# A fused long-convolution and MLP block on one Trainium2 core: the same operations in another sequence

## The chip, the core and the metric

The kernel runs on one core of one Trainium2 chip. Its time is the device time of one execution in microseconds (us). A core has five engines with an instruction queue each: TensorE (PE in the profile, with its weight loads as PEld), VectorE (DVE), ScalarE (ACT), GpSimd (POOL) and SyncE (SP). They run side by side and meet at semaphores only; each executes its own instructions strictly in the order in which they were written. DMA transfers are started by an instruction on SP, ACT or POOL and are then carried out by 16 DMA engines.

## What is computed

```python
x  = A_q                                   # 1 x 2048 x 640, bf16
xn = _layernorm(x)
# A: depthwise 4-tap convolution of k, times v, then a 2048-long convolution by FFT
k_shift = sum over t of k_pad[:, t:t+S, :] * shift_k[:, ks-1-t]
kv = k_shift * v
y  = irfft(rfft(pad(kv)) * rfft(pad(ssm_k)))[:S] + kv * ssm_D
s  = xn * y
# B: MLP 640 -> 1728 -> 640
g  = silu(gelu(xn @ w1 + b1) @ w2 + b2)
return x + s * g
```

## The kernel before

**Tiles.** The 2048 rows are 16 tiles of 128 rows and 640 columns. For the MLP they form four chunks of four tiles (chunk 0 is tiles 0 to 3). The FFT is done by matmuls in two factors, with two round trips through DRAM scratch (`scrK`, `scrU` after the first factor, `scrC` after the products), in 8 groups.

**Operations.** The kernel is a plan of about 700 named operations. Each name is made of a kind and its indices:

- Layer norm of tile i: `bn` (statistics, DVE), `rs0` to `rs5` (the reciprocal root for a group of tiles, POOL: `rs0` is tile 0, `rs1` tile 1, `rs2` tiles 2 and 3, `rs3` tiles 4 to 7, `rs4` 8 to 11, `rs5` 12 to 15), `xn` (normalize, DVE), `xt` (transpose, PE), `xe` (copy out of PSUM, ACT or DVE).
- MLP: `f1_c_r_ft` is one output block of the first matrix (five matmuls of 512 columns; for chunk 0 the first five blocks come in halves), `ge_...` its gelu on ACT with the bias `b1f`, `f1h` and `geh` the half-height last block. `f2_i_h` is half the columns of tile i of the second matrix (14 matmuls of 320 columns), `si_i` its silu on ACT, `gx_i` the product with `xn` on DVE. ACT must load another function table where gelu and silu alternate (line 687).
- Bias: `b1l` is the DMA of the 3.5 KB of `b1` into `b1r`, and `b1c` converts it into `b1f`, which every gelu reads.
- 4-tap convolution: `kv0` to `kv4`, long DVE operations, `kv4_4` the last.
- FFT: `K1_i`, `U1_i` and their remainders `K1r`, `U1r` are the first factor for the filter and for the signal (PE); `Ke`, `Ue`, `Ker`, `Uer` copy them out of PSUM; `Ks`, `Us` store to scratch, `KL`, `UL` load back. `K2`, `U2`, `X2` are the second factor, `Kf`, `Uf` their copies. `pr`, `pq` are the complex products (DVE). `i1`, `i1r` and `ie`, `ir` are the first inverse factor and its copies, `cs` stores to `scrC`, `cl` loads it, `i2` is the last factor, `ym`, `ad` combine on DVE, `os` stores the output.

**What sets the order.** A string `ORDER` lists every operation once. `Plan.emit` walks through it and writes each operation's instructions into the queue of its engine, so the list is the order on each engine. A token is `name/engine@slots`: after the slash an engine other than the default one (A is ACT, D is DVE, G is POOL, S is SP; N stays on PE but issues each matmul as two of 64 output rows), after the at sign the numbers of the PSUM banks and other buffers that the operation takes:

```python
for token in tokens:
    ...
    o = self.by_name[name]
    e = code[e] if e else o.engs[0]
    ...
    if o.func is not None and o.func != self.table:
        if o.func is not ACT.Sin:
            preload(o.func)
    ...
    o.fn(e)
```

An operation that takes a bank waits for the last reader of that bank. DMAs of SP and ACT share eight completion semaphores in turn, so that a DMA waits for the one eight places before it. `wu0` to `wu5` are four matmuls each on a zero tile, which occupy PE before data has arrived.

In the list of before, `b1l/A` is the first token, `b1c/D` stands behind the first four `xe`, and `rs1`, `rs2`, `rs0` behind `rs3` on POOL.

Of the kernel before, what the change touches and what calls it, by code (L numbers as in the profile page):

```python
# [700 lines left out]
f1_1_0_0@0 kl2 xn0 gte1/A kv0_1a f1_1_0_7@1 xe1/A w2l1 ge_1_0_0 Da xt0@3 sm3 f1_0_1_1@4.1 kv0_2m@0 xe0/A f1h_1@5  # L701
ge_1_0_5 f1h_0@7 ge_1_0_7 kv0_2a f1_0_1_0/N@2 ge_0_1_1 f1_0_0_2/N@0 geh_1 f1_0_0_8/N@3 ge_0_1_0 kv0_3m@0 ge_0_0_2
geh_0 f1_0_0_5/N@6 vl1 ge_0_0_8 kv0_3a K1r_2@4.2 K1_9@0 K1_11@2 Ke_9/A f1_0_0_6@7 vl3 kv0_4 Ker_2/A f1_1_0_4@0 Ke_11/A
kv1_0@0 K1_10@4 f1_0_0_3@1 ge_0_0_6 f1_1_0_1@2 bn14 ge_0_0_3 ge_1_0_4 kv1_1m@1 f1_0_1_2@3 Ke_10/A f1_0_1_3@7 ge_0_0_5
f1_0_0_7@1 kv1_1a ge_0_1_3 ge_0_1_2 f1_1_0_11@0 ge_1_0_1 bn13 ge_0_0_7 f1_0_1_4@4 ge_1_0_11 f1_1_0_8@5 bn15 ge_0_1_4
bn12 K1_2@6.0 K1r_0@2 Ke_2/A K1_8@0 f1_0_0_12@4 kv1_2m@1 Ker_0/A f1_0_0_10@6 ge_1_0_8 rs5 Ke_8/A f1_0_0_4@7 f1_0_0_9@2
ge_0_0_10 kv1_2a one0 Ks_2 vl2 ge_0_0_4 f1_0_0_0@3 ge_0_0_9 K1_0@0 xn13 K1_1@6 kv1_3m@1 Ke_0/A f1_0_0_1@5 f1_0_0_11@2
Ke_1/A kv1_3a K1_3@0 ge_0_0_11 ge_0_0_1 ge_0_0_12 f2_2_1@6.0 kv2_0@1 ge_0_0_0 f2_2_0 xn12 kv1_4 f2_7_1@4.1 xn15 si_2
kv2_1m@0 Ke_3/A Ks_0 U1_0@2.2 kv2_1a U1_3@6 xl4 Ue_0/A U1_1@0 kl3 f2_7_0 Ue_1/A xn14 kv2_2m@0 Ue_3/A U1r_0@2 U1_2@0
si_7 kv2_2a Uer_0/A Ue_2/A gx_2 f2_4_1@6.0 kv2_3m@0 U1_7@4.0 U1_6@2 ss Us_0 U1_4@0 f2_4_0 KL0@0 Ue_6/A KL1@1 sx kv2_3a  # L710
Ue_7/A xt13@2.0 gx_7 si_4 f2_5_1@4.1 kv2_4 xe13/A Ue_4/A kv3_0@0 U1r_1@6 U1_5@2 kv3_1m@1 Uer_1/A U1_11@0.2 f2_5_0 gx_4
Ue_5/A kv3_1a bn11 Us_1 gt0@6 KL3@4 f2_1_1@2.0 kv3_2m@1 KL7@2 gte0/A KL2@5 kv3_2a Ue_11/A kv3_3m@1 U1_8@6 U1_10@0
Ue_8/A f2_1_0 kv3_3a si_5 kv3_4 Ue_10/A kv4_0@1 xt15@6 xt12@7 si_1 gx_5 K2_0_0@4 kv4_1m@0 K2_1_0@0 Kf_0_0/A f2_3_0@2.1
kv4_1a Kf_1_0/A kv4_2m@0 xe15/A U1_9@4 kv4_2a U1r_2@0 f2_3_1 Uer_2/A kv4_3m@0 xe12/A kv4_3a Ue_9/A xt14@6 gx_1
f2_6_1@0.0 xe14/A bn8 Us_2 si_3 kv4_4 U1_12@4.0 gx_3 U1r_3@6 Ue_12/A U1_14@2 bn10 f2_6_0 Uer_3/A bn9 Ue_14/A rs4
U1_15@4 U1_13@6 si_6 f1_3_0_5@2.0 Ue_13/D Ue_15/A K2_3_0@0 xn8 K2_7_0@6 Us_3 xn10 f1_3_0_7@3 xn9 Kf_7_0/D xt8@4.1
ge_3_0_7 f1_3_0_4@5 Kf_3_0/D ge_3_0_5 xt10@6 xe8/A f1_3_0_9@7 gx_6 ge_3_0_4 xe10/D xn11 K2_0_1@2 ge_3_0_9 K2_2_0@0
K2_7_1@4 Kf_2_0/D Kf_0_1/A f1_3_0_0@6 UL0@6 UL1@3 Kf_7_1/A xt11@7 UL2@8 f1_3_0_1@2 UL6@9 ge_3_0_0 KL6@10 xe11/A UL3@7
K2_2_1@0 K2_3_1@4 ge_3_0_1 xt9@3 Kf_3_1/D f1_3_0_12@6 Kf_2_1/D f1_3_0_3@7 ge_3_0_12 xe9/D K2_1_1@4 ge_3_0_3 U2_0_0@0
# [10 lines left out]
Kf_5_0/A f1_2_0_5@3 ge_2_0_8 gx_0 U2_5_0@6 pq_4_0@1 ge_2_0_5 X2_5@0 pr_4_0@2 Uf_5_0/A i1_6@4.2 pq_4_1 Kf_5_2/A  # L730
f1_2_0_7@6 ie_6_0/D Uf_5_2/A ie_6_1/A U2_7_0@0 pq_5_1 K2_5_1@4 pq_5_0 ge_2_0_7 f1_2_0_1@7 pr_4_1@0 Kf_5_1/A
f1_2_0_12@2 Uf_7_0/D ge_2_0_1 i1r_2@4.6 ge_2_0_12 pq_6_0@3 U2_7_1@0 ir_4_0/D ir_4_1/A X2_7@2 ir_5_1/A ir_5_0/D
Uf_7_1/A pq_6_1 i1_4@6.4 Uf_7_2/D Kf_7_2/D f2_11_0@0.0 ie_4_1/A pq_7_0 pq_7_1 ie_4_0/A pr_7_0@1 U2_5_1@2 cs_4/S
# [48 lines left out]
```

## Time and profile before

| | us |
|---|---|
| median of 3 runs (lowest, highest) | 184.49 (184.37, 184.64) |
| the profiled execution, its own time | 184.11 |
| span of the profiled execution | 182.3 |
| busy: PE / DVE / ACT / POOL | 174.7 / 159.5 / 144.6 / 24.2 |
| DMA moved | 50.64 MB, 278 GB/s on average |

The span runs from the first to the last recorded instruction or transfer; the execution's own time lies 1.8 us around it. A busy time is the time in which an engine had at least one instruction running; matmuls are pipelined, so that two records overlap and PE at its peak shows a mean of about twice the distance between two starts.

### The profile page before, as it was taken

Reading aid. Unit: us, or ns where it says so; the run is one execution under the profiler, and the core shown is the slowest. Engines: PE = TensorE matmul, PEld = TensorE weight load, DVE = VectorE, ACT = ScalarE, POOL = GpSimd, SP = SyncE. Lnnn points to the kernel's source line nnn. Section 1 sums busy time; section 2 is a strip of 40 time slices with the busy share of each in tenths; the row PEclk is TensorE's granted clock in tenths of the full one; section 3 lists DMA queues with packets and bytes.
Section 4 is the critical chain, followed back from the end, with each engine's and each line's share of the span. In section 5 each row is a group of like instructions: output and inputs, shape, how many; then the busy total and the mean of one; then the engine's idle time right before and its main releaser. Section 6 shows DMA issues by size and latency. Waiting matters only on the chain.

```text
span 182.3 us, 5237 instructions
## 1 busy us (share of the span) xinstructions
PE 174.7 (96%) x2220; PEld 102.4 (56%) x2221; DVE 159.5 (87%) x246; ACT 144.6 (79%) x211; POOL 24.2 (13%) x52
## 2 busy tenths in 40 slices
...
GB/s 168 417 415 422 409 416 429 412 422 205 347 88 304 424 377 372 378 264 117 226 342 363 170 132 166 291 240 182 224 68 5 286 168 174 405 413 405 65 241 158
DMA packets 20713, 50.64 MB, mean 278 GB/s; under 512 B 1745, under 2 KB 15314, under 8 KB 19282
## 3 DMA queue, kind: packets, MB, share of 16 engines
...
## 4 chain that ended last, share of the span: by engine, by line
PE 71%; DVE 17%; DMA 5%; ACT 3%; issue 2%; POOL 1%; SPq 0%; POOLq 0%; DVEq 0%; ACTq 0%
PE ps L436 31%; PE ps L477 21%; DVE xn L669 6%; PE ps L564 5%; PE ps L605 4%; PE ps L350 4%; PE ps L414 3%; DMA v<-scrC 2%; DVE x L673 2%; DMA scrC<-v 2%; DVE stats L382 2%; DVE v L181 1%; DVE xn L494 1%; DVE x L681 1%; PE ps L451 1%
## 5 line engine op out<-in xcount | busy, mean ns | idle before, releaser
L477 PE MATMUL ps<-w,hT 128*64 128x320 bf16 (+4 forms) x658 | 65.6, 294 | 0.0
L436 PE MATMUL ps<-xnT,w 128*128 128x512 bf16 (+3 forms) x315 | 61.3, 359 | 0.2 <-ACT sl L490 0.2
L477 PEld LDWEIGHTS <-hT 128*64 128x64 bf16 (+3 forms) x658 | 46.8, 105 | 16.0 <-issue 3.9
L436 PEld LDWEIGHTS <-w 128*128 128x128 bf16 (+1 forms) x315 | 26.6, 100 | 28.7 <-issue 7.5
L181 ACT CAST st<-ps 128x1024 bf16<-128x1024 f32 x37 | 36.3, 1023 | 4.5 <-PE ps L350 3.8
L440 ACT ACTIVATE hT<-ps,b1f 128x512 bf16<-128x512 f32 (+1 forms) x57 | 35.4, 661 | 3.6 <-PE ps L436 3.2
L490 ACT ACTIVATE sl<-ps 128x640 bf16<-128x640 f32 (+2 forms) x18 | 11.7, 651 | 18.8 <-PE ps L477 14.5
L181 ACT CAST k<-ps 128x1024 bf16<-128x1024 f32 (+2 forms) x20 | 16.8, 869 | 2.6 <-issue 1.5
L530 DVE TENSOR_TENSOR lat<-lat 128x2560 bf16<-128x2560 bf16 (+1 forms) x15 | 18.4, 1224 | 0.4
L527 DVE TENSOR_TENSOR lat<-k,lat 128x2560 bf16<-128x2560 bf16 (+1 forms) x15 | 18.1, 1209 | 0.1
L181 DVE CAST v<-ps 128x1024 bf16<-128x1024 f32 (+2 forms) x12 | 12.4, 1042 | 4.1 <-PE ps L564 3.1
L494 DVE TENSOR_TENSOR xn<-xn,sl 128x640 bf16<-128x640 bf16 (+2 forms) x18 | 8.2, 457 | 8.3 <-ACT sl L490 8.2
L669 DVE TENSOR_TENSOR xn<-ps,xn 128x640 bf16<-128x640 f32 x16 | 12.7, 818 | 1.4 <-PE ps L665 1.3
L382 DVE BATCH_NORM_STATS2 stats<-x 128x6 f32<-128x320 bf16 x32 | 13.7, 469 | 0.0
L181 ACT CAST v<-ps 128x1024 bf16<-128x1024 f32 (+2 forms) x18 | 13.0, 765 | 0.4 <-PE ps L564 0.4
L687 ACT ACT_TABLE_LOAD x10 | 12.8, 1283 | 0.2
L181 DVE CAST k<-ps 128x512 bf16<-128x512 f32 (+2 forms) x13 | 11.0, 849 | 0.8 <-PE ps L564 0.4
L589 DVE TENSOR_TENSOR st<-k 128x512 bf16<-128x512 bf16 (+1 forms) x12 | 9.3, 819 | 0.1
L605 PE MATMUL ps<-st,I 32*64 32x512 bf16 x256 | 8.8, 380 | 0.3 <-ACT v L181 0.2
L397 POOL TENSOR_SCALAR rstd<-mv 128x4 f32<-128x4 f32 (+2 forms) x6 | 2.4, 406 | 47.2 <-DVE mv L383 47.2
L333 PE MATMUL ps<-hT 128*128 128x512 bf16 x23 | 7.1, 464 | 1.2 <-DVE hT L215 1.2
L404 DVE TENSOR_SCALAR xn<-x,mv,rstd 128x640 bf16<-128x640 bf16 x16 | 6.8, 459 | 1.2 <-POOL rstd L398 0.9
...
## 6 DMA issues: line engine op xcount, KB each, us to landing
...
```

What stands on the lines that cost most here:

```text
L181: (nc.scalar.copy if e == "ACT" else nc.vector.tensor_copy)(out=out_, in_=in_)
L382: nc.vector.bn_stats(out=stats[:, i, h, :], in_=x_t[:, i, h * H:(h + 1) * H])
L436: nc.tensor.matmul(out=pb.v[us, 0:b - a], lhsT=w1_t[:, ft, t, us], rhs=xnTb[c].v[:, a // P:b // P, t, :], start=(t == 0), stop=(t == DT - 1))
L440: nc.scalar.activation(out=hTb[c].v[:, ft, a:b], in_=pb.v[:, 0:b - a], func=ACT.Gelu_apprx_tanh, bias=b1_f[:, ft:ft + 1], scale=1.0)
L477: nc.tensor.matmul(out=o[us, 0:b - a], lhsT=hTb[c].v[0:M, ft, q * P + us.start:q * P + us.stop], rhs=w2_t[0:M, ft, a:b], start=(ft == 0), ...
L490: nc.scalar.activation(out=o_, in_=i_, func=ACT.Silu)
L494: op("gx_" + nm, "DVE", lambda e, a=a, b=b: nc.vector.tensor_tensor(out=xn_t[:, i, a:b], in0=xn_t[:, i, a:b], in1=s_.v[:, a:b], op=ALU.mul ...
L527: op("kv%d_%dm" % (r, j), "DVE", lambda e, i=i, n=n, j=j, t=t, wb=wb: nc.vector.tensor_tensor(out=t.v[:, 0:n, :], in0=k_t[:, i + 3 - j:i + ...
L530: op("kv%d_%da" % (r, j), "DVE", lambda e, n=n, t=t, a=a: nc.vector.tensor_tensor(out=a.v[:, 0:n, :], in0=a.v[:, 0:n, :], in1=t.v[:, 0:n, ...
L605: nc.tensor.matmul(out=pb[j // 2].v[64 * a:64 * a + 64, j % 2, :], lhsT=I1_t[32 * j:32 * j + 32, m, :], rhs=o[w][32 * j:32 * j + 32, a, r, ...
L669: op("ym_%d" % i, "DVE", lambda e, i=i, pb=pb: nc.vector.tensor_tensor(out=xn_t[:, i, :], in0=pb.v.rearrange("p a b -> p (a b)")[:, 0:D], ...
L687: nc.scalar.activation(out=tab[:], in_=cst[:], func=func)
```

## The change

Only the string `ORDER` differs. The operations, their code, the buffers and their sizes are the same; the sequence on every engine is another one, 62 operations sit on another engine, and 16 matmul blocks change between whole and half issue (N). The heads, a piece from the middle and the ends of both lists:

```diff
--- before.py
+++ after.py
 ORDER = """
-b1l/A grid xl3 zz xl1 wu2@0 fix sm0 wm1 Kl4 Kl2 c0 w1l1 wm2 wm0/G xl0 wu0@1 w1l2 wq2 sm1 ws2 wq1 wu3@2 sm2 Dl/A bn5
-w1l3 ws1 xl2 wu1@3 bn6 bn7 skl K1_12@4.0 K1_13@6 wu4@0 Ke_13/A bn4 K1r_3@2 Ke_12/A kl0 K1_4@0.2 K1_15@6 Ker_3/D rs3
-Ke_15/A K1r_1@4 vl0 wq0 K1_5@2 w1l0 Ke_4/A id wu5@6 xn4 xn5 ws0 xn6 xt4@7.0 xn7 xt5@6 Kl0 xt6@0 xe4/D xe5/A xt7@1 Kl3
-xe6/D gt1@7 Ke_5/A xe7/D b1c/D bn1 K1_6@0 f1_1_0_6@6.0 Ke_6/A Ker_1/D rs1 f1_1_0_3@2 xn1 bn3 f1_1_0_2@3 ge_1_0_6
-ge_1_0_3 bn2 K1_14@0 K1_7@4 ge_1_0_2 f1_1_0_10@6 Ke_7/A bn0 rs2 f1_1_0_12@2 ge_1_0_10 Ks_1 rs0 xn3 kl1 xn2 xl5
-f1_1_0_9@3 ge_1_0_12 kv0_1m@0 one1 Ke_14/A xt3@4.1 xt2@5 f1_1_0_5@6 ge_1_0_9 kv0_0@1 Ks_3 Kl1 xe3/A w2l0 xt1@2 xe2/A
...
-pr_0_0@3 X2_1@0 si_0 pr_0_1@0 U2_2_0@4 U2_1_1@2 Kf_1_2/A f1_2_0_3@6.1 Uf_1_1/A Uf_1_2/D KL4@0 pq_1_1 i1_0@2.0 Uf_2_0/D
...
-ge_2_0_0 X2_2@4 cs_1/S Uf_3_0/D X2_4@6 Uf_2_2/A X2_3@0 Kf_2_2/A Kf_4_2/D KL5@6 U2_3_1@2 Uf_3_2/A f1_3_0_6@4 pq_2_0@2
-Kf_3_2/A pq_2_1 Uf_4_2/D Uf_3_1/A f1_3_0_8@5 pq_3_1 pq_3_0 ge_3_0_6 pr_2_1@0 i1r_1@0.6 ge_3_0_8 UL7@3 f1_2_0_2@2
...
-pr_7_1@0 i1r_3@4.6 Uf_5_1/A f2_11_1 ir_7_1/A pr_5_0@2 ir_6_0/A ir_7_0/A ir_6_1/A cs_6/S pr_5_1@3 i1_7@2.4 f2_8_0@6.1
-ie_7_0/A ie_7_1/D cs_7/S i1_5@2.4 si_11 ie_5_0/A gx_11 f1h_3@0 ie_5_1/D f2_8_1/N cs_5/S geh_3 f2_10_1/N@2.0
-f1_3_0_10/N@1 si_8 cl_0@4 gx_8 cl_2@7 cl_3/G@8 f2_10_0/N cl_1/G@0 cl_7/G@10 f2_9_1/N@4.1 si_10 cl_6/G@2 gx_10 cl_4/G@6
-i2_1@6 cl_5/G@1 i2_0@2 ge_3_0_10 ym_1 f2_9_0/N ad_1 ym_0 os_1 i2_5@0 ad_0 si_9 i2_4@6 ym_5 f2_14_0/N@2.0 ym_4 ad_5
...
+grid xl3 zz Kl4 wu5@0 fix c0 wm0/G wm1 Kl2 xl0 wm2 w1l3 w1l0 wu4@1 sm0 w1l1 wq1 xl2 wq2 ws1 id sm1 wu1@2 wq0 ws2 sm2
+xl1 bn6 ws0 wu0@3 bn4 w1l2 K1_14@4.0 K1_13@6 bn5 Ke_14/A wu3@0 kl0 Ke_13/A bn7 K1_12@2 K1_15@4 skl K1_4@0.2 Ke_12/A
+wu2@6 sm3 rs3 Ke_15/D Ke_4/A K1r_3@2 K1_6@6 K1_5@4 xn6 Ker_3/A xn7 xt6@0.0 xn4 xt7@1 xe6/A xn5 xt4@2 xt5@3 xe7/A xe4/D
+gt1@0 xe5/D b1l/A gt0@1 gte1/D Ke_6/A f1_1_0_12@2.0 bn2 Ke_5/A f1_1_0_10@3 bn3 b1c K1r_1@6 bn0 rs2 K1_7@4 Ker_1/A
+f1_1_0_4@0 xl5 Kl1 bn1 vl0 rs0 f1_1_0_3@6 Ks_3 Kl3 rs1 xn0 Kl0 f1_1_0_8@7 ge_1_0_4 xn3 one1 ge_1_0_3 xn1 xn2 one0
+f1_1_0_1@0 ge_1_0_10 Dl kv0_0@0 ge_1_0_8 kl1 xt3@6.1 ge_1_0_1 f1_1_0_2@3 ge_1_0_12 kv0_1m@1 xt0@7 ge_1_0_2 f1_1_0_11@0
...
+pr_0_0@1 xe9/D U2_1_1@0 si_0 X2_1@6 pr_0_1@2 Uf_1_1/A U2_2_0@2 f1_2_0_6@4.1 Kf_1_2/D Uf_2_0/A Uf_1_2/D f1_2_0_10@5
...
+pr_2_0@0 X2_3@0 ge_2_0_0 X2_2@2 Uf_3_0/A Uf_3_2/D f1h_2@4 Kf_3_2/D Kf_2_2/A f1_3_0_8/N@5 Uf_2_2/A pq_3_0@1 pq_3_1
+geh_2 X2_4@6 pq_2_0 pq_2_1 ge_3_0_8 U2_3_1@0 Uf_4_2/D K2_6_0@2 UL5@6 Uf_3_1/A f1_3_0_6@4 KL5/G@0 Kf_4_2/D Kf_6_0/A
+pr_3_0@3 i1r_1@6.0 f1_2_0_2@5 ir_3_1/A ir_2_1/A pr_3_1@1 ge_3_0_6 i1_2@2.0 ir_3_0/A ge_2_0_2 UL7@1 ir_2_0/D f1_3_0_2@4
...
+ir_7_0/A pr_7_1@1 f2_11_0 Uf_5_1/A ir_6_1/A ir_6_0/D ir_7_1/D cs_6/S gx_1 i1_7@0.4 pr_5_0@3 si_11 f2_8_1@6.0 ie_7_0/A
+pr_5_1@2 ie_7_1/A i1_5@2.0 cs_7/S f2_8_0 ie_5_0/D ie_5_1/A gx_11 cs_5/S f2_10_0@4.1 si_8 gx_8 f2_9_1@0.0 cl_0@8 cl_2@4
+cl_3/G@3 f2_10_1 cl_1/G@9 cl_7/G@7 cl_6/G@5 f1_3_0_10@2 si_10 cl_4/G@2 gx_10 f1h_3@3 i2_1@6 i2_0@4 ym_1 ge_3_0_10
+f2_9_0/N geh_3 ad_1 ym_0 i2_5@6 ad_0 i2_4@2 ym_5 f2_14_0/N@4.1 si_9 ad_5 ym_4 i2_7@6 gx_9 i2_6@0 ym_7 i2_3@2 f2_14_1/N
...
```

Counted over both lists: 1024-element copies out of PSUM, 65 on ACT and 23 on DVE before, 70 and 18 after; 512-element copies 9 and 7 before, 6 and 10 after; 256-element copies 12 and 4 before, 9 and 7 after; ACT's table loads 11 before, 9 after; DMAs issued by POOL 8 before, 13 after; matmuls on PE 36 fewer, since other blocks are issued in halves. `b1c` goes from DVE to POOL, `gte1` from ACT to DVE.

More of the change, by code (lines that the diff above doesn't have):

```diff
@@ L700 @@
-f1_1_0_9@3 ge_1_0_12 kv0_1m@0 one1 Ke_14/A xt3@4.1 xt2@5 f1_1_0_5@6 ge_1_0_9 kv0_0@1 Ks_3 Kl1 xe3/A w2l0 xt1@2 xe2/A
[L701 to L719, printed above, removed]
@@ L720 @@
-X2_0@2 Kf_1_1/A f2_0_0@6.1 Uf_0_2/D Uf_0_0/A Kf_0_2/D pq_0_1@2 pq_0_0 U2_1_0@4 U2_0_1@2 Uf_1_0/A f2_0_1 Uf_0_1/D
-pr_0_0@3 X2_1@0 si_0 pr_0_1@0 U2_2_0@4 U2_1_1@2 Kf_1_2/A f1_2_0_3@6.1 Uf_1_1/A Uf_1_2/D KL4@0 pq_1_1 i1_0@2.0 Uf_2_0/D
-f1_2_0_6@7 ge_2_0_3 ie_0_0/D ie_0_1/A f1_2_0_11@4 pq_1_0 ge_2_0_6 pr_1_1@1 i1r_0@2.0 ge_2_0_11 X2_6@6 ir_0_0/A
-ir_1_1/D ir_1_0/A U2_6_0@4 ir_0_1/D Kf_6_2/A U2_2_1@2 pr_1_0@0 f1h_2@0 Uf_6_2/A f1_2_0_9/N@1 Uf_2_1/A Uf_6_0/D UL4@1
-cs_0/S i1_1@6.2 ge_2_0_9 pr_2_0@3 geh_2 U2_6_1@4 f1_2_0_10@1 ie_1_1/A Uf_6_1/D f1_2_0_0@0 ie_1_0/D ge_2_0_10 U2_3_0@2
@@ L730 @@
[L730 to L733, printed above, removed]
-pr_7_1@0 i1r_3@4.6 Uf_5_1/A f2_11_1 ir_7_1/A pr_5_0@2 ir_6_0/A ir_7_0/A ir_6_1/A cs_6/S pr_5_1@3 i1_7@2.4 f2_8_0@6.1
@@ new lines @@
+wu2@6 sm3 rs3 Ke_15/D Ke_4/A K1r_3@2 K1_6@6 K1_5@4 xn6 Ker_3/A xn7 xt6@0.0 xn4 xt7@1 xe6/A xn5 xt4@2 xt5@3 xe7/A xe4/D
+gt1@0 xe5/D b1l/A gt0@1 gte1/D Ke_6/A f1_1_0_12@2.0 bn2 Ke_5/A f1_1_0_10@3 bn3 b1c K1r_1@6 bn0 rs2 K1_7@4 Ker_1/A
+f1_1_0_4@0 xl5 Kl1 bn1 vl0 rs0 f1_1_0_3@6 Ks_3 Kl3 rs1 xn0 Kl0 f1_1_0_8@7 ge_1_0_4 xn3 one1 ge_1_0_3 xn1 xn2 one0
+f1_1_0_1@0 ge_1_0_10 Dl kv0_0@0 ge_1_0_8 kl1 xt3@6.1 ge_1_0_1 f1_1_0_2@3 ge_1_0_12 kv0_1m@1 xt0@7 ge_1_0_2 f1_1_0_11@0
+xe0/A kv0_1a xt1@2 gte0/A f1_1_0_9@3 xe1/A kv0_2m@1 f1_1_0_5@7 ge_1_0_9 xe3/A xt2@1 kv0_2a f1_0_0_2@2.1 xe2/A
```

41 lines of the change are left out of this document (33 added, 8 removed).

## The prediction

> **What bounds the kernel now.** I read the page first, then busy time in stretches of 5 us, then the head in order of time.
>
> ```profile
> span 182.3 us, 5237 instructions
> PE 174.7 (96%) x2220; PEld 102.4 (56%) x2221; DVE 159.5 (87%) x246; ACT 144.6 (79%) x211; POOL 24.2 (13%) x52
> PE 71%; DVE 17%; DMA 5%; ACT 3%; issue 2%; POOL 1%; SPq 0%; POOLq 0%; DVEq 0%; ACTq 0%
> ```
>
> PE is busy 96% of the span and carries 71% of the chain that ended last: TensorE is the bound, and its work is the same in both lists. A new sequence can only change the time in which PE stands still, or runs filler. Where that is, the stretches show (PE's busy time is the second number, then PEld, DVE, ACT, POOL, and DMA share and GB/s last):
>
> ```profile
> 0.00:5.00 5.00, 3.83 (x11) 1.44 (x12) 3.84 (x15) 1.81 (x2) 3.66 (x16) 1.00 0.65 191
> 5.00:10.00 5.00, 3.92 (x34) 1.56 (x34) 4.86 (x14) 4.20 (x7) 3.86 (x13) 1.00 1.03 416
> 10.00:15.00 5.00, 4.54 (x47) 2.63 (x43) 4.85 (x14) 4.78 (x7) 1.50 (x3) 1.00 1.02 416
> 15.00:20.00 5.00, 5.00 (x25) 1.98 (x24) 4.75 (x13) 4.97 (x8) 2.13 (x6) 1.00 1.01 412
> 100.00:105.00 5.00, 4.67 (x96) 2.37 (x95) 4.86 (x6) 4.94 (x9) 0.00 (x0) 1.00 0.59 176
> 105.00:110.00 5.00, 4.87 (x108) 2.58 (x107) 5.00 (x8) 5.00 (x10) 0.00 (x0) 1.00 0.33 120
> 115.00:120.00 5.00, 4.50 (x90) 2.00 (x77) 5.00 (x9) 4.83 (x11) 0.00 (x0) 1.00 0.89 293
> 145.00:150.00 5.00, 4.76 (x80) 3.67 (x80) 2.31 (x3) 4.94 (x8) 0.00 (x0) 1.00 0.52 183
> 155.00:160.00 5.00, 4.89 (x72) 3.91 (x70) 2.81 (x5) 4.46 (x7) 1.47 (x3) 1.00 1.01 406
> ```
>
> From 15 to 100 us no stretch has PE idle (the first of them, 15 to 20, is shown). In the FFT stage, 100 to 140, the three stretches with the most idle have 0.33 + 0.13 + 0.50 = 0.96 us, the tail 0.24 + 0.11 = 0.35. So a better packing behind the head can gain about 1.3 us at the most; a loss has no such bound. The remaining room is the head, where filler covers the wait for data.
>
> **The head.** DVE must finish the statistics of tiles 4 to 7 before anything of the MLP can start:
>
> ```profile
> 5.38 0.88 DVE L382 BATCH_NORM_STATS2 stats<-x 128x6 f32<-128x320 bf16 x2
> 9.89 1.05 POOL L398 TENSOR_TENSOR rstd<-rstd,mhalf 128x4 f32<-128x4 f32 x1
> 10.48 0.42 DVE L238 TENSOR_SCALAR w<-w 128x512 int32<-128x512 int32 x1
> 10.98 1.51 DVE L404 TENSOR_SCALAR xn<-x,mv,rstd 128x640 bf16<-128x640 bf16 x4
> 14.17 3.41 PE L436 MATMUL ps<-xnT,w 128*128 128x512 bf16 x15
> 17.52 0.39 PE L350 MATMUL ps<-xn,W 64*128 64x512 bf16 x2
> 7.84 3.76 ACT L181 CAST st<-ps 128x1024 bf16<-128x1024 f32 x4 [0.80 <-PE ps L350]
> 13.17 1.02 ACT L181 CAST st<-ps 128x1024 bf16<-128x1024 f32 x1
> 16.77 1.83 ACT L440 ACTIVATE hT<-ps,b1f 128x512 bf16<-128x512 f32 x3
> 21.30 0.72 PE L414 MATMUL ps<-ident,xn 128*128 128x128 bf16 x10
> ```
>
> The new list puts `wq0` (0.42, the row at 10.48) ahead of `bn6`, so `rs3`, `xn` and the first `f1` come about 0.4 later: 14.5 instead of 14.17. By then PE has done one `K1` and one `gt` more and one `K1r` less, about 0.3 us of work. Net **+0.1 us** (between -0.3 and +0.4).
>
> **The bias.** This is where I see the price. Before, `b1l` is ACT's first instruction, and `b1c` runs on DVE when its data is long there. In the new list `b1l` stands on ACT behind two `xe`, and `b1c` on POOL ahead of `rs2`, `rs0`, `rs1`. So POOL waits for that DMA, behind it the layer norm of tiles 0 to 3, behind `xn0` all of DVE's `kv`, behind `xn3` PE at `xt3`; and ACT's first gelu waits for `b1c` too.
>
> ```profile
> 0.72 0.41 ACTq L304 DMA_DIRECT2D b1r<-in_b  x1
> b1r<-in_b ACTq DMA_DIRECT2D x1, 3.5 KB, 4.7
> 5.21 0.50 ACTq L304 DMA_DIRECT2D Dr<-in_ssm_D  x1
> q10 hardware_dynamic: 144, 0.00, 3.2%
> q1 hardware_dynamic: 290, 1.21, 101.1%
> q10 hardware_dynamic: 2, 0.00, 1.0%
> w<-in_w SPq DMA_DIRECT2D x1, 800.0 KB, 8.5
> ```
>
> When is it issued? Before, ACT has run three pairs of W, four 1.0-us copies and one `xe` by 13.17. The new list needs one copy more (1.02) and no longer has the 0.80 of idle at 7.84, since `ws0` fills it: `b1l` goes out at 13.17 + 1.02 - 0.80 = 13.4.
>
> How long does it take? Before, 4.7 us (q10 is ACT's queue; the three queue rows are the windows 2.4 to 4.9, 5.7 to 8.6 and 8.6 to 9.0). Its packets moved from 2.4 on, 1.7 after the issue, while the DMA engines were filling. `Dr`, issued at 5.21 into saturated engines, moved nothing in 5.7 to 8.6, where q1 took 101%, and began 3.4 after its issue. At 13.4 to 18 the engines are as full as then (the loads ahead in the new list are 6.6 MB by their sizes, which from 2.4 on take until 18 at the 0.416 MB per us of the stretches above). So I add the 1.7 by which `Dr` began later: 4.7 + 1.7 = **6.4 us**, landing at 19.8. The ends are 4.7 and the 8.5 of a load in SP's loaded queue.
>
> The Trainium skill, "DMA: Bandwidth & Descriptors", section "Anatomy of one DMA — SWDGE (gpsimd) path", gives a fixed cost of about 2.0 us plus bytes over 436 GB/s. The 4.7 us here for 3.5 KB disagrees; by that rule the bias would land at 15.4, ahead of every need, and the sum below would lose its largest term.
>
> What does that delay?
>
> ```profile
> 4.57 0.19 POOL L270 CAST st<-st 128x1 f32<-128x1 int32 x1 [0.54 <-DVE st L260]
> 18.53 0.23 POOL L397 TENSOR_SCALAR rstd<-mv 128x2 f32<-128x2 f32 x1 [2.60 <-DVE mv L383]
> 19.53 0.23 POOL L397 TENSOR_SCALAR rstd<-mv 128x1 f32<-128x1 f32 x1
> 19.84 0.62 POOL L398 TENSOR_TENSOR rstd<-rstd,mhalf 128x1 f32<-128x1 f32 x1
> ```
>
> From landing to `xt3`: `b1c` 0.3 with its wake-up, `rs2` 1.0 (18.53 to 19.53), `rs0` 0.9 (19.53 to 20.46), `xn0` and `xn3` 0.4 each (1.51 for four), hand-over 0.1: 3.1 us. So `xn3` is there at 19.8 + 3.1 = 22.9. PE would reach `xt3` at 14.5 + 7.1 = 21.6: six `f1` at 1.12 (three between 14.17 and 17.52) are 6.7, `K1r_1` and `K1_7` together 0.4 (as the row at 17.52). The loss is 22.9 - 21.6 = **1.3 us**; none if the DMA takes 5.1 or less, 3.4 at 8.5. DVE loses more, about 2 us on `kv`; its list up to `kv4_4` is as long as before's without the `rs5` wait, so `U1r_3`, which needs `kv4_4`, still comes no later than PE does. Nothing between 15 and 80 us covers a PE stall, since PE has no idle time there to give back.
>
> **The FFT stage.** Between `Uer_3` and `ie_5`, ACT gets five 1024-element copies more and three 512s, three 256s and an `xe` less; DVE the reverse.
>
> ```profile
> L181 ACT CAST v<-ps 128x1024 bf16<-128x1024 f32 x9 | 9.2, 1021 | 0.4 <-PE ps L564 0.4
> L181 ACT CAST v<-ps 128x512 bf16<-128x512 f32 x5 | 2.7, 604 | 0.0
> L457 ACT ACTIVATE hT<-ps,b1f 64x256 bf16<-64x256 f32 x8 | 3.7, 465 | 0.1
> 115.83 0.41 PE L564 MATMUL ps<-v,F 64*32 64x512 bf16 x8 [0.49 <-DVE v L181]
> ```
>
> That is 5 x 1.02 - 3 x 0.60 - 3 x 0.39 - 0.7, about 1.4 us more on ACT, which was at 4.8 to 5.0 of 5 there already. Following banks by hand, two places wait. `U2_2_1` and `U2_6_0` wait for `ge_2_0_11` and the first `ir`, about 0.8 together. And `f1_3_0_6` and `i1r_1` wait for `geh_2` and `Uf_3_1`: behind `f1h_2` ACT still has `Kf_2_2`, `Uf_2_2`, `geh_2` (2 x 0.465), a gelu (0.6) and `Uf_3_1`, 3.7 us, and PE only two `f1` and three short blocks, 3.1; with what ACT is already behind, 1.0. Together 1.8, and the 0.96 of before goes, which would be +0.8; since each of these waits is a difference of two sums of ten rows, I take half: **+0.4 us**, between -1.0 (all of before's idle gone) and +1.4 (all of ACT's extra work on the path).
>
> **The tail.** Before, `ie_5_1` stood on DVE behind `gx_11`, which waited for ACT's table load and `si_11`:
>
> ```profile
> 147.54 0.49 DVE L494 TENSOR_TENSOR xn<-xn,sl 128x640 bf16<-128x640 bf16 x1 [1.86 <-ACT sl L490]
> ```
>
> Now `si_11` runs earlier, `ie_5_0` is ahead of `gx_11`, and `cs_5` goes about 1.2 earlier; but the `f2` blocks between `i1_5` and `i2_1` are as many as before and fill that time, so only PE's 0.35 of idle goes: **-0.3 us**. The two table loads saved and DVE's lighter load lie beside PE and give nothing else.
>
> ```profile
> L436 PE MATMUL ps<-xnT,w 128*128 128x512 bf16 x215 | 51.3, 380 | 0.2 <-ACT sl L490 0.2
> L436 PE MATMUL ps<-xnT,w 128*64 128x512 bf16 x40 | 4.8, 379 | 0.0
> ```
>
> The other issue of 16 blocks costs nothing: 51.3 / 215 = 0.239 us a whole matmul, 4.8 / 40 = 0.120 a half.
>
> **Sum.** 0.1 + 1.3 + 0.4 - 0.3 = +1.5 us. The profiled execution took 184.11, so the new one would take 185.6 there; it lies 0.4 under the median of the runs, 184.49, and on that median I forecast **186.0 us**.
>
> **Rivals.** *The bias comes in time* (20%): it lands within 5.1 us, as 4.7 before. Then 0.1 + 0.4 - 0.3 = 0.2, 184.7 us, and no difference either way that a measurement would show. For it: the transfer is tiny and on a queue of its own. Against it: `Dr`. The skill's rule of 2.0 us stands on this side.
> *Packed better* (8%): the bias in time and the FFT stage's idle gone: 0.1 - 1.0 - 0.3 = -1.2, 183.3 us. For it: DVE loses copies there; against it: ACT gains them.
> *ACT alone* (10%): the bias in time, but ACT's 1.4 fully on PE's path: 0.1 + 1.4 - 0.3 = 1.2, 185.7 us; it decides when PE waits for ACT in most stretches of 100 to 140.
> The forecast itself has 62%.
>
> **Numbers.** Two in ten may lie outside: low 184.1 (the bias in time and a little gained), high 187.9 (landing after 8 us, 2.9 in place of 1.3, and 0.3 more in the FFT stage). About 0.2%, 0.37 us, is what a measurement of this kernel can tell from no change. Slower by more: the forecast nearly whole (60) and ACT alone (10), 70%; within: 12%, most of the first rival and 2 of the forecast; faster: 18%, the second rival and the better half of the first.
>
> **What would show it.** In the profile of the changed kernel: `b1r` issued by ACT at 13 to 14 us, with over 5.1 us to landing; POOL waiting for it ahead of line 397; DVE idle at about 19 to 22 us until `rstd`; PE idle over 1 us in 20 to 25 us. If PE shows none there, the step on the landing is wrong; if the FFT stage has under 0.8 us of PE idle, the one on ACT; and if PE's idle is as forecast and the time not, PE was not the bound.

## The result, and the profile after

| | us |
|---|---|
| before, median of 4 runs (lowest, highest) | 184.43 (184.03, 184.64) |
| after, median of 4 runs (lowest, highest) | 189.00 (187.76, 189.16) |
| after over before | 1.0238, 95% interval 1.0215 to 1.0261 |
| profiled execution after: own time, span | 188.93, 187.2 |

The new order is slower, as forecast, but by 4.6 us in place of 1.5, outside the range (184.1 to 187.9). Five of the kernels below (a_b1l_first, a_b1c_behind, a_kl4_behind, a_slots and a_kl6_pool) have some runs about 2 us longer at a mean clock of 0.99, of which no trace was kept; their profiled executions have 0.995 or more, and their traces are compared by these.

The page of after, busy times and chain, and its stretches (columns as before):

```profile
span 187.2 us, 5162 instructions
PE 176.6 (94%) x2185; PEld 100.1 (53%) x2185; DVE 158.9 (85%) x248; ACT 142.3 (76%) x205; POOL 25.8 (14%) x57
DVE 40%; PE 33%; DMA 12%; ACT 6%; issue 4%; POOL 2%; SPq 0%; DVEq 0%; POOLq 0%
20.00:25.00 5.00, 3.33 (x19) 1.44 (x18) 2.06 (x4) 3.58 (x6) 3.89 (x9) 1.00 0.95 320
80.00:85.00 5.00, 4.64 (x47) 2.99 (x40) 4.90 (x8) 4.04 (x5) 0.00 (x0) 1.00 0.95 339
100.00:105.00 5.00, 3.05 (x37) 1.79 (x35) 4.53 (x7) 1.49 (x3) 0.00 (x0) 1.00 0.99 338
115.00:120.00 5.00, 5.00 (x136) 2.49 (x135) 4.17 (x6) 4.76 (x7) 0.11 (x1) 1.00 0.93 281
145.00:150.00 5.00, 5.00 (x96) 2.92 (x81) 4.98 (x7) 4.45 (x7) 0.00 (x0) 1.00 0.75 262
```

PE has 71% of the chain before and 33% after; DMA went from 5% to 12%. PE has new idle time in three places: 1.67 us in 20 to 25, 0.36 in 80 to 85 (none in either before) and 1.95 in 100 to 105 (0.33 before). The first two follow from the bias, the third does not stand in the prediction. The idle time of before in 145 to 150 (0.24) is gone, and that in 115 to 120 (0.50) has moved: 0.38 stand in 120 to 125.

The bias, in order of time on ACT, POOL, DVE and PE:

```profile
13.16 0.39 ACTq L304 DMA_DIRECT2D b1r<-in_b  x1
b1r<-in_b ACTq DMA_DIRECT2D x1, 3.5 KB, 7.5
20.73 0.19 POOL L314 CAST b1f<-b1r 128x14 f32<-128x14 bf16 x1 [8.97 <-DMA b1r<-in_b]
20.96 3.58 ACT L440 ACTIVATE hT<-ps,b1f 128x512 bf16<-128x512 f32 x6 [1.17 <-POOL b1f L314]
22.83 2.29 DVE L404 TENSOR_SCALAR xn<-x,mv,rstd 128x640 bf16<-128x640 bf16 x4 [3.75 <-POOL rstd L398]
21.70 1.24 PE L436 MATMUL ps<-xnT,w 128*128 128x512 bf16 x5 [0.91 <-DMA x<-in_x]
23.69 0.45 PE L414 MATMUL ps<-ident,xn 128*128 128x128 bf16 x5 [0.75 <-DVE xn L404]
83.08 0.29 PE L361 MATMUL ps<-v,W 64*128 64x128 bf16 x4 [0.36 <-DVE v L532]
```

The load takes 7.5 us, POOL stands idle for 8.97 us until it has landed, DVE for 3.75 until POOL is done, and PE waits twice: at the sixth `f1` (21.70) and at `xt3` (23.69). The first wait is put down to a load of `x` that had landed long before; it ends when the first gelu has released its bank (20.96 and about 0.7), as an experiment below shows with the right name: the sixth `f1`, `f1_1_0_1`, takes bank 0, which the first gelu, `ge_1_0_4`, has yet to read. The last row is `U1r_3`, which waits for `kv4_4`.

The third place, on PE and on the DMA queues (window 85 to 106); the first two rows are of before, the others of after:

```profile
98.58 0.41 PE L564 MATMUL ps<-k,F 64*32 64x512 bf16 x8
k<-scrU SPq DMA_DIRECT2D x1, 640.0 KB, 5.6
103.16 0.41 PE L564 MATMUL ps<-k,F 64*32 64x512 bf16 x8 [1.95 <-DMA k<-scrU]
lat<-scrU POOLq DMA_DIRECT2D x1, 640.0 KB, 8.4
k<-scrU SPq DMA_DIRECT2D x1, 640.0 KB, 10.5
v<-scrK POOLq DMA_DIRECT2D x1, 640.0 KB, 9.9
```

`U2_1_0` waits for `UL1` (`k<-scrU`), which took 5.6 us before, in time for its reader, and takes 10.5 now. `UL2` and `KL6` were behind it on SP's queue and are now on POOL's, beside it:

```diff
-UL0@6 UL1@3 Kf_7_1/A xt11@7 UL2@8 f1_3_0_1@2 UL6@9 ge_3_0_0 KL6@10
+UL0@6 ge_3_0_12 UL1@3 UL2/G@8 xe10/A KL4@9 xt11@1 UL6@10 KL6/G@7
```

### The profile page after: what moved, and what is told of

Same layout as the page of the kernel before. It is cut to its first block, busy times and chain, and to the rows that moved or that the text cites. A ratio compares the mean times of both kernels' runs of the same rounds, so it can differ in the third digit from the quotient of the medians.

```text
span 187.2 us, 5162 instructions
## 1 busy us (share of the span) xinstructions
PE 176.6 (94%) x2185; PEld 100.1 (53%) x2185; DVE 158.9 (85%) x248; ACT 142.3 (76%) x205; POOL 25.8 (14%) x57
## 4 chain that ended last, share of the span: by engine, by line
DVE 40%; PE 33%; DMA 12%; ACT 6%; issue 4%; POOL 2%; SPq 0%; DVEq 0%; POOLq 0%
PE ps L477 18%; DVE lat L530 10%; DVE lat L527 9%; DMA k<-scrU 6%; PE ps L436 6%; DMA b1r<-in_b 4%; PE ps L605 4%; DVE stats L382 4%; DVE v L532 3%; DVE lat L523 3%; PE ps L665 2%; DMA scrU<-st 2%; DVE st L589 2%; PE ps L564 2%; ACT hT L440 2%
## 5 line engine op out<-in xcount | busy, mean ns | idle before, releaser
L477 PE MATMUL ps<-w,hT 128*128 128x320 bf16 (+4 forms) x602 | 65.2, 293 | 0.1
L477 PEld LDWEIGHTS <-hT 128*128 128x128 bf16 (+2 forms) x602 | 44.6, 103 | 18.5 <-issue 4.1
L181 ACT CAST st<-ps 128x1024 bf16<-128x1024 f32 x37 | 35.6, 1022 | 6.2 <-PE ps L350 3.5
L440 ACT ACTIVATE hT<-ps,b1f 128x512 bf16<-128x512 f32 (+1 forms) x57 | 34.6, 665 | 2.6 <-POOL b1f L314 1.2
L181 ACT CAST k<-ps 128x1024 bf16<-128x1024 f32 (+2 forms) x21 | 17.8, 870 | 4.8 <-PE ps L564 3.5
L181 ACT CAST v<-ps 128x1024 bf16<-128x1024 f32 (+2 forms) x17 | 13.5, 822 | 1.4 <-PE ps L605 1.4
L181 DVE CAST k<-ps 128x1024 bf16<-128x1024 f32 (+2 forms) x12 | 10.0, 841 | 2.7 <-ACT hT L440 1.4
L404 DVE TENSOR_SCALAR xn<-x,mv,rstd 128x640 bf16<-128x640 bf16 x16 | 7.3, 487 | 5.6 <-POOL rstd L398 5.4
L687 ACT ACT_TABLE_LOAD x8 | 10.3, 1283 | 0.1
L333 PE MATMUL ps<-hT 128*128 128x512 bf16 x24 | 8.6, 524 | 1.3 <-DVE hT L215 1.2
L181 ACT CAST lat<-ps 128x1024 bf16<-128x1024 f32 (+2 forms) x10 | 8.4, 854 | 0.1
```

The source lines that it names most:

```text
L181: (nc.scalar.copy if e == "ACT" else nc.vector.tensor_copy)(out=out_, in_=in_)
L333: nc.tensor.matmul(out=pb.v, lhsT=hT_t[1][:, 0, 0:P], rhs=hT_t[1][:, 0, :], start=True, stop=True)
L440: nc.scalar.activation(out=hTb[c].v[:, ft, a:b], in_=pb.v[:, 0:b - a], func=ACT.Gelu_apprx_tanh, bias=b1_f[:, ft:ft + 1], scale=1.0)
L477: nc.tensor.matmul(out=o[us, 0:b - a], lhsT=hTb[c].v[0:M, ft, q * P + us.start:q * P + us.stop], rhs=w2_t[0:M, ft, a:b], start=(ft == 0), ...
L687: nc.scalar.activation(out=tab[:], in_=cst[:], func=func)
```

## The experiments

Each kernel is timed against the kernel before on the same chip; the interval is that of the ratio to it. Names that begin with a_ are edits of the changed order, with b_ of the order before. "Both edits" is the kernel a_both.

### The two costs, undone one by one

**a_b1l_first**: the bias load first, as before.

```diff
-grid xl3 ... xe5/D b1l/A gt0@1
+b1l/A grid xl3 ... xe5/D gt0@1
```

> The changed order with one token moved: b1l (on ACT) is the first one again, as in the order before. The theory that the late bias costs PE its two waits behind it (0.91 us at f1 while ACT's first gelu waits for b1f, 0.75 at xt3 while POOL and then DVE are late) and the 0.36 at U1r_3 (kv4_4 late) expects 1.7 to 2.0 us less than the changed kernel: about 187.1, with b1r landing before 6 us and no PE wait over 0.2 us in 20 to 25. The rival, that this loss is made up elsewhere because the load of U1 for group 1 ends last anyway, expects less than 0.5 us: 188.6 or more.

Measured: 186.37 (186.02 to 188.57), ratio 1.0137 (1.0096 to 1.0179): 2.6 less than after. PE has no idle time left in 20 to 25 and in 80 to 85; the wait for `UL1` stays (1.83). The gain is more than the 2.0 of the three waits as recorded (0.91 + 0.75 + 0.36); what each wait really delays is read below.

**a_b1c_behind**: `b1l` stays late, POOL alone is let past.

```diff
-b1c K1r_1@6 bn0 rs2 ... rs0 f1_1_0_3@6 Ks_3 Kl3 rs1
+K1r_1@6 bn0 rs2 ... rs0 f1_1_0_3@6 Ks_3 Kl3 rs1 b1c
```

> The changed order with b1c moved on POOL from ahead of rs2 to behind rs1; b1l stays late. If POOL being blocked is what costs (the prediction's step), xt3 is reached in time and only the wait of the gelus stays: 0.75 us less, about 188.2, and up to 1.1 less if kv4_4 is in time too. If the gelus' wait for b1f is the whole cost, nothing changes (189.0), since b1r lands at 20.7 as before and b1c follows at once.

Measured: 188.19 (187.01 to 189.26), ratio 1.0205 (1.0168 to 1.0242); the profiled execution took 187.52, against 188.93 after. Its PE:

```profile
21.73 1.24 PE L436 MATMUL ps<-xnT,w 128*128 128x512 bf16 x5 [0.94 <-ACT hT L440]
22.80 0.44 PE L414 MATMUL ps<-ident,xn 128*128 128x128 bf16 x5
```

The wait at the sixth `f1` stays and is now named after the gelu; the one at `xt3` is gone, 0.89 earlier than 23.69, and the one at `U1r_3` with it. In the traces every matmul behind `U1r_3` is 1.41 to 1.55 us earlier, more than the 0.75 to 1.1 expected. Both routes cost: POOL's and the gelu's.

**a_ul_sp**: the two loads on SP again, the bias late.

```diff
-UL2/G@8 ... KL6/G@7
+UL2@8 ... KL6@7
```

> The changed order with UL2 and KL6 on SP's queue again in place of POOL's, tokens where they are; the bias stays late. The theory that the two loads on POOL's queue take their share of the bandwidth from UL1, which U2_1_0 waits for 1.95 us, expects UL1 to land 5 to 6 us after its issue in place of 10.5 and 1.7 to 2.0 us less: about 187.1. The rival, that UL1 is late because all loads of this stage are (Us_3 is issued 2.6 us later than before and everything behind it is bound by bytes), expects the wait to stay above 1.5 us and the time within 0.4 of 189.0.

Measured: 186.83 (186.41 to 186.98), ratio 1.0125 (1.0109 to 1.0141): 2.2 less than after. `UL1` lands 6.9 us after its issue, and PE does not wait for it. The rival, that all loads of this stage are late, fell.

**a_both**: the two edits together.

> Both edits: b1l first, UL2 and KL6 on SP. If the two costs are separate and both as large as their waits, they add up: 3.4 to 4.0 us less than the changed kernel, 185.0 to 185.6, and 0.5 to 1.1 us stay above the kernel before (later last stores about 0.7, the FFT stage the rest). If one hides behind the other, the sum is under 2.5 us: 186.5 or more. If the prediction's FFT step (ACT's copies, +0.4) and its tail (-0.3) are right as they stand, the time is within 0.4 of the kernel before's.

Measured: 184.06 (183.82 to 184.35), ratio 0.9979 (0.9970 to 0.9988): 4.9 less than after, against 2.6 + 2.2 = 4.8. The costs add up, to more than the 3.4 to 4.0 expected, and without them the new order is 0.2% faster than the order before. Its PE and its load:

```profile
21.70 0.44 PE L414 MATMUL ps<-ident,xn 128*128 128x128 bf16 x5
80.30 0.39 PE L361 MATMUL ps<-v,W 64*128 64x128 bf16 x8
98.35 0.40 PE L564 MATMUL ps<-k,F 64*32 64x512 bf16 x8
k<-scrU SPq DMA_DIRECT2D x1, 640.0 KB, 6.7
95.00:100.00 5.00, 4.91 (x92) 3.09 (x92) 4.37 (x8) 3.63 (x6) 0.00 (x0) 1.00 1.07 365
105.00:110.00 5.00, 4.87 (x109) 2.15 (x94) 5.00 (x8) 4.99 (x11) 0.88 (x1) 1.00 0.22 55
115.00:120.00 5.00, 4.58 (x99) 2.16 (x96) 4.72 (x10) 4.96 (x11) 0.76 (x1) 1.00 0.42 129
135.00:140.00 5.00, 4.83 (x126) 2.87 (x124) 4.37 (x9) 4.63 (x8) 0.00 (x0) 1.00 0.02 3
```

PE has the same 2185 matmuls in the same order in both kernels, so the k-th start of one can be set beside the k-th of the other. After is later by 1.08 at the sixth `f1`, 1.99 at `xt3` (23.69 against 21.70), 2.66 at the second half of `U1r_3` (83.08 against 80.42, inside the row at 80.30), 4.81 at `U2_1_0` (103.16 against 98.35), and 4.79 at the end: bias 1.08 + 0.91 + 0.67 = 2.66, `UL1` 2.15, and nothing else.

### The same costs put into the order before

**b_bias_late**:

```diff
-b1l/A grid ... gt1@7 Ke_5/A xe7/D b1c/D bn1
+grid ... gt1@7 b1l/A Ke_5/A xe7/D b1c bn1
```

> The kernel before with the bias as late as in the changed one: b1l on ACT ahead of Ke_5, and b1c on POOL ahead of rs1 in place of DVE. The theory that the late bias first costs PE the bank that a waiting gelu holds: only three f1 are ahead of f1_1_0_10, which needs the bank of ge_1_0_6; with b1r at 20.7 that gelu ends at 21.6 in place of 18, so 3.5 to 3.9 us more, 187.9 to 188.3. The prediction's step, that the cost is the late xt3 (rs1, rs2, rs0 and xn behind b1c, xn3 at about 24 for xt3 at 21.3), expects 2.5 to 2.9 us more and PE's wait at xt3 rather than at f1_1_0_10.

Measured: 189.48 (189.06 to 190.86), ratio 1.0298 (1.0268 to 1.0329): 5.2 more, above both. PE, and its clock (the column after POOL's):

```profile
21.43 5.08 PE L436 MATMUL ps<-xnT,w 128*128 128x512 bf16 x15 [3.30 <-ACT hT L440]
20.00:22.00 2.00, 0.57 (x2) 0.25 (x2) 0.43 (x2) 1.31 (x3) 0.98 (x3) 0.88 1.04 407
22.00:24.00 2.00, 2.00 (x6) 0.71 (x5) 1.93 (x8) 1.72 (x3) 0.00 (x0) 0.50 0.53 214
24.50:25.00 0.50, 0.50 (x3) 0.15 (x1) 0.47 (x2) 0.00 (x0) 0.50 (x1) 0.57 0.80 328
```

The wait is where the gelu theory puts it, at `f1_1_0_10`, and 3.30 us long. Behind it the granted clock is half from 21.5 to 24.9, and the 15 matmuls (three `f1`) take 5.08 us, where the 15 of before that the prediction shows took 3.41: 1.67 more. 3.30 + 1.67 = 4.97 of the 5.2. The Trainium skill, "TensorE: Matmul & The Clock Gate", "Part 1: The HAM clock gate", says that the array falls to half rate after an idle window of about 3.4 us and needs a busy one to come back; this trace agrees to about 0.1 us, 3.30 us idle and then 3.4 us at 0.50. One such dip costs half of 3.4, so 1.7 us, and lowers the mean clock over 187 us by 0.009. One of the six runs took 189.12 us at a mean clock of 0.999, which this sum does not explain.

**b_ul_pool**:

```diff
-UL2@8 ... KL6@10
+UL2/G@8 ... KL6/G@10
```

> The kernel before with UL2 and KL6 on POOL's queue in place of SP's, tokens where they are. The theory that loads on POOL's queue make one of the sixteen parts of UL1 arrive late (15 parts 6.1 to 6.6 us after its issue, the last 10.5, in the changed kernel) expects UL1, issued at 90.05, to end at about 100.5; the first matmul that reads it (98.58 before) would wait 2.0 us, and the time be 186.0 to 186.5. The rival, that the two queues only share the bandwidth, puts UL1 at 96.7, ahead of its reader, and expects no change: 184.4, within 0.3.

Measured: 184.61 (184.16 to 185.10), ratio 1.0013 (1.0001 to 1.0024). The expectation that loads on POOL's queue make a part of `UL1` late in any order fell here: the same edit costs 0.2 us in the order before. `UL1` takes 7.1 and is in time for `U2_1_0`:

```profile
k<-scrU SPq DMA_DIRECT2D x1, 640.0 KB, 7.1
98.72 0.41 PE L564 MATMUL ps<-k,F 64*32 64x512 bf16 x8
```

The trace has a landing for each of the 16 parts of a load. Those of `UL1`, from its issue on, in us:

```
                   parts 1 to 15     part 16   read by PE
before             5.2 to 5.6        5.6        8.5
after              6.1 to 6.6       10.5       10.5
a_both             5.2 to 5.6        6.8        8.4
b_ul_pool          6.1 to 6.7        7.1        8.5
```

Beside the loads on POOL's queue the first fifteen parts are 0.8 to 1.1 later. That alone would cost nothing, since `U2_1_0` comes 8.4 to 8.6 us behind the issue in all of these orders (after: 103.16 less its wait of 1.95). It is the one part 3.9 us behind the others for which PE waits. The Trainium skill, "DMA: Bandwidth & Descriptors", "Queues, rings and completion order", says that a load is spread over up to 16 engines and that each of them takes turns between the queues that have work for it; its section "Why a DMA increments its semaphore by 16 and not by 1" says that only the full 16 means that all data has landed. The trace agrees in the 16 landings and in PE's wait for the last of them; turns between queues would fit the 0.8 to 1.1, and why one part should be behind by 3.9 us those sections do not say.

### What makes the last part late

**a_ul_act**: both edits, but `UL2` and `KL6` on ACT's queue (the kernel's two lines that issue such loads now allow ACT too).

```diff
-Kf_3_0/A ... ge_3_0_7 xn11 f1_3_0_4@0 UL0@6 ge_3_0_12 UL1@3 UL2@8 ... KL6@7
+Kf_3_0/A ... UL2/A@8 ge_3_0_7 xn11 f1_3_0_4@0 UL0@6 ge_3_0_12 KL6/A@7 UL1@3
```

> The kernel with both edits (b1l first, UL2 and KL6 not on POOL), but with UL2 and KL6 on ACT's queue in place of SP's: UL2 behind Kf_3_0, KL6 behind the next two gelus. If it is POOL's queue that makes one part of UL1 late, UL1 ends 6 to 8 us after its issue and the time stays at 184.0 to 184.8 (ACT has two issues of about 0.4 us more). If any second queue does it, UL1 ends after 10 us and the time is 185.8 to 186.5.

Measured: 186.02 (185.90 to 186.24), ratio 1.0097 (1.0083 to 1.0112). A second queue that is not POOL's costs as well, but in another way: the two loads went out at 89.47 and 90.01, 0.3 and 0.8 earlier than on POOL in a_b1l_first and the first ahead of `UL0`, and all parts of `UL1` are late, 15 of them 8.5 to 8.8 us after the issue and the last 9.9.

```profile
99.91 0.41 PE L564 MATMUL ps<-k,F 64*32 64x512 bf16 x8 [1.37 <-DMA k<-scrU]
```

The time is that of the second theory, its mechanism is not: no single part is far behind (1.1 us), and all of `UL1` is late when another load goes first.

**a_ul2_pool** and **a_kl6_pool**: both edits, but one load on POOL.

> The kernel with both edits, but UL2 alone on POOL's queue. UL2 is issued ahead of UL1's turn there, KL6 behind it. If the late part takes two loads on POOL, the time stays at 184.0 to 184.5 with UL1 in 6.5 to 8 us. If UL2, which overlaps all of UL1, does it alone, UL1 ends after 9 to 10.5 us and the time is 185 to 186.5.

> The kernel with both edits, but KL6 alone on POOL's queue. If the late part of UL1 takes two loads on POOL, UL1 ends in 6.5 to 8 us, ahead of the 8.5 at which it is read, and the time stays at 184.0 to 184.5. If KL6 alone does it, UL1 ends after 9 to 10.5 us and the time is 185 to 186.5.

Measured: 184.43 (184.18 to 185.24), ratio 1.0008 (0.9995 to 1.0020), and 185.33 (184.56 to 187.71), ratio 1.0052 (1.0037 to 1.0068). The first row is of UL2 alone on POOL, the others of KL6 alone:

```profile
99.08 0.41 PE L564 MATMUL ps<-k,F 64*32 64x512 bf16 x8 [0.54 <-DMA k<-scrU]
...
v<-scrU SPq DMA_DIRECT2D x1, 640.0 KB, 6.4
96.08 0.41 PE L564 MATMUL ps<-v,F 64*32 64x512 bf16 x8 [0.89 <-ACT hT L440]
```

With `UL2` alone the last part comes 9.1 us after the issue, 2.0 behind the fifteenth, and PE waits 0.54: half of the lag by one load, and about a quarter of the wait. So neither theory held whole: the lag needs no second load, but most of the cost does. `KL6` alone was no clean test. It no longer stands behind `UL2`, which waits for the store of `Us_3`, so POOL issued it at 86.20, beside that store; `UL0` then took 6.4 us (4.3 with both edits), and PE waits 0.89 behind that, while `UL1` landed after 7.7, in time. The view names a gelu there; `UL0`'s last part landed at 96.04, just ahead of 96.08.

**a_kl4_behind**: `b1l` first, `UL2` and `KL6` on POOL, and SP's loads in the sequence of b_ul_pool.

```diff
-UL1@3 UL2/G@8 xe10/A KL4@9 xt11@1 UL6@10 KL6/G@7
+UL1@3 UL2/G@8 xe10/A xt11@1 UL6@10 KL6/G@7 KL4@9
```

> The changed kernel with b1l first; UL2 and KL6 stay on POOL, but KL4 on SP moves from between UL1 and UL6 to behind UL6 and KL6, so that SP's loads stand as in the kernel before with UL2 and KL6 on POOL, where UL1 ended 7.1 us after its issue and nothing was lost. If what follows UL1 on SP's queue makes its last part late, UL1 now ends in 7 to 8 us and the time is 184.0 to 184.6. If it is the two loads on POOL whatever SP has behind UL1, its last part comes after 10 us again and the time is 186.1 to 186.6.

Measured: 187.31 (186.28 to 188.66), ratio 1.0165 (1.0125 to 1.0205), the profiled execution 186.60; `UL1` takes 10.5 again, and PE waits 1.90. What follows `UL1` on SP's queue is not the reason.

**a_slots** and **b_slots**: the buffers of the loads exchanged.

```diff
 a_kl4_behind                                b_ul_pool
-UL6@10 KL6/G@7 KL4@9                        -KL6/G@10 UL3@7
+UL6@9 KL6/G@10 KL4@7                        +KL6/G@7 UL3@10
```

> The changed kernel with b1l first and SP's and POOL's loads as in the kernel before with UL2 and KL6 on POOL, their buffers now too: UL6 in buffer 9, KL6 in 10, KL4 in 7. If the buffers that the loads write decide whether the last part of UL1 is late, UL1 ends 7 to 8 us after its issue and the time is 184.0 to 184.6. If it is something else of the list, it ends after 10 us and the time is 186.1 to 186.7.

> The kernel before with UL2 and KL6 on POOL and with KL6 in buffer 7 and UL3 in buffer 10, as KL6 has it in the changed kernel. If the buffers decide, UL1's last part comes 10 us after its issue, its reader waits 1.5 to 2.0 us, and the time is 186.0 to 186.6. If not, UL1 ends after 7.1 us and the time is 184.6.

Measured: 186.19 (185.94 to 187.76), ratio 1.0123 (1.0080 to 1.0166), and 184.32 (183.94 to 184.58), ratio 1.0003 (0.9992 to 1.0014). The loads' rows, first of a_slots, then of b_slots:

```profile
k<-scrU SPq DMA_DIRECT2D x1, 640.0 KB, 10.4
...
k<-scrU SPq DMA_DIRECT2D x1, 640.0 KB, 6.6
```

The buffers do not decide either. All five profiles of the changed order with both loads on POOL have the late part (10.4 to 10.5), both of the order before have not (6.6 and 7.1), at the same sequence of issues and nearly the same distances.

The loads on POOL's queue show the other side. In those five profiles the last part of `UL2` lands 8.3 to 8.4 us after its issue and that of `KL6` 9.7 to 9.9; in the two without the late part it is 9.0 to 9.1 and 10.3 to 10.4, while the fifteenth parts agree to 0.2 in all seven (7.8 to 7.9 and 9.0 to 9.2). So where the last part of `UL1` is late, the last parts of POOL's loads are early by 0.4 to 0.8. That is what one DMA engine would do that serves POOL's queue ahead of `UL1` in one order and behind it in the other. It is not shown that this is so, since the trace does not name the engine of a part, and what of the order sets it stays open.

### The last stores

In all profiles of the changed order but the last one below, the span ends 3.1 to 3.3 us after the last DVE operation (after: 187.2 - 183.90), in that of before 182.3 - 179.74 = 2.6:

```profile
179.50 0.24 DVE L681 TENSOR_TENSOR x<-xn,x 128x160 bf16<-128x160 bf16 x1
183.66 0.24 DVE L681 TENSOR_TENSOR x<-xn,x 128x160 bf16<-128x160 bf16 x1
```

The first row is of before, the second of after.

**a_both_store**: both edits, `os_15_1` on SP in place of ACT.

> The kernel with both edits, and os_15_1, the last store, on SP as in the kernel before, in place of ACT behind os_12. The span ends 3.2 us after the last DVE operation there and 2.6 before. If the queue of the last store is the reason, 0.3 to 0.65 us less than with both edits (184.06): 183.4 to 183.8, which would be the fastest of all. If the end is set by the stores that are still queued on SP, no change: 184.0.

Measured: 184.31 (183.84 to 184.91), ratio 1.0000 (0.9988 to 1.0012). There is no gain, and the span still ends 3.1 us after the last DVE operation; the queue of the last store is not the reason.

**a_both_os10**: both edits, two stores behind their own data.

```diff
-ad_10 si_12 ad_11 gx_12 f2_15_1/N si_15_2 os_11/A gx_15_2 ad_15_2 ad_12 os_15_2 si_15_1 os_10 os_12/A
+ad_10 os_10 si_12 ad_11 os_11 gx_12 f2_15_1/N si_15_2 gx_15_2 ad_15_2 ad_12 os_15_2 si_15_1 os_12/A
```

> The kernel with both edits, and two stores earlier: os_10 and os_11 directly behind the ad that makes their data, both on SP; in the changed order os_10 stands on SP behind os_15_2, and os_11 on ACT behind a silu, so that 400 KB are issued in the last microsecond of the span's work, against 320 before. If that is why the span ends 3.2 us after the last DVE operation in place of 2.6, 0.3 to 0.6 us less than with both edits: 183.4 to 183.8. If the end is the delay of the last store alone, no change: 184.0.

Measured: 183.81 (183.53 to 184.04), ratio 0.9967 (0.9953 to 0.9981). The span ends 181.8 - 179.04 = 2.8 after the last DVE operation, 0.4 less, as the bytes in the last microsecond let expect:

```profile
178.80 0.24 DVE L681 TENSOR_TENSOR x<-xn,x 128x160 bf16<-128x160 bf16 x1
```

It has the lowest median of all and is faster than the order before by 0.3%. Against a_both the gain is about 0.2 us by the two ratios, whose intervals overlap, so that the runs alone do not show it.

## Why the prediction was right or wrong

**Head, +0.1: right.** The first `f1` starts at 14.58 (14.5 forecast), and without the bias `xt3` is reached at 21.70 (21.6). In the sum below the head comes to 0, within the stated ends.

**Bias, +1.3: right place, measured 2.66.** The issue at 13.16 (13.4), and 3.0 us from landing to `xt3` (3.1), held. Three steps failed. First, the landing took 7.5 us, not 6.4, within its ends; that is 20.7 in place of 19.8, and 1.99 at `xt3` in place of 1.3. Second, half of this is no longer POOL's: 1.08 is lost ahead of it at the sixth `f1`, where the bank of a waiting gelu is missing. The prediction named the gelu's wait and left out the bank that the gelu holds. Third, the sentence that `U1r_3` would come "no later than PE does" failed: DVE lost more than PE, `kv4_4` came late, 0.67. The rival that the bias comes in time is refuted, and so are the other two, which rest on the same condition. The rule of 2.0 us, which the prediction put on the first rival's side, is given by the Trainium skill ("DMA: Bandwidth & Descriptors", "Anatomy of one DMA — SWDGE (gpsimd) path") for DMAs that GpSimd issues; this one went out on ACT's queue and took 7.5.

**FFT stage, +0.4: wrong, measured -0.3 for the term itself, inside its stated ends, and +2.15 for one that was not in it.** From 95 to 145 us a_both has 0.09 + 0.13 + 0.42 + 0.17 = 0.81 of PE idle, before 0.33 + 0.13 + 0.50 + 0.16 = 1.12 (the last from the stretch of before that the prediction does not show):

```profile
135.00:140.00 5.00, 4.84 (x121) 2.99 (x120) 4.83 (x10) 4.33 (x7) 0.00 (x0) 1.00 0.00 0
```

ACT's 1.4 us more is not on PE's path: at the two named places after waits 0.21 (`f1_3_0_6`) and 0.17 (`i1r_1`) in place of 1.0, and at `U2_2_1` and `U2_6_0` at most 0.13 in place of 0.8. Differences of sums of ten rows gave waits that did not come, and by the prediction's own sign (under 0.8 us of PE idle in this stage; 0.72 in 100 to 140 of a_both) the step on ACT fails. The larger failure is the list of moved work: POOL issues 13 DMAs in place of 8, as counted ahead of the prediction, and the prediction followed copies and banks alone. `UL2` and `KL6` on another queue ran beside `UL1`, the load that PE needs next. Had it followed them, shared bandwidth would have put `UL1` at 6.1 to 6.7 us, ahead of its reader; the late part could not be read from the trace of before. That only 2.9 us lay before between the landing (95.69) and the reader (98.58) could, and made it the load to watch.

**Tail, -0.3: right**, 0.24 + 0.11 of idle in 145 to 160 went to none, **but the last stores are missing**: +0.65, as `os_10`, `os_12` and the last two go out together. Issuing `os_10` and `os_11` earlier took 0.4 of it away in the trace of a_both_os10; the rest is not explained.

**Sum.** 0 + 2.66 - 0.3 + 2.15 - 0.35 + 0.65 = 4.8, and the spans differ by 187.2 - 182.3 = 4.9. Without bias and `UL1`, packing gains about 0.65 (in a_both the last matmul ends 0.64 earlier than before, at 178.21 against 178.84), and in the traces the stores give it back: both spans are 182.3. By the medians about 0.3 us of it stays.
